# A new written order for the first two chunks of a fused attention and MLP kernel

## The chip, the cores and the metric

The kernel runs on one core of one Trainium2 chip. Its time is the device time of one execution in microseconds (us); of several runs the median is taken. A core has five engines with an instruction queue each, worked off in order: TensorE (PE: matrix products, with weight loads shown as PEld), VectorE (DVE), ScalarE (ACT), GpSimd (POOL) and SyncE (SP, which here only issues transfers). They meet at semaphores: an instruction waits until another engine or a transfer has raised one.

## The reference

Attention whose keys are limited to the query's hash bucket, then a layer norm and an MLP with a residual, on 4 batches of 8 heads, 768 positions, 64 dimensions a head:

```python
q_bits = (np.einsum('bhsd,dk->bhsk', q, proj) > 0).astype(np.int64)
k_bits = (np.einsum('bhsd,dk->bhsk', k, proj) > 0).astype(np.int64)
mask = q_bucket[:, :, :, None] == k_bucket[:, :, None, :]
scores = scale * np.matmul(q, k.transpose(0, 1, 3, 2))
scores = np.where(mask, scores, -1000000000.0)
attn = np.exp(scores - np.max(scores, axis=-1, keepdims=True))
attn = attn / (np.sum(attn, axis=-1, keepdims=True) + 1e-09)
x = np.matmul(attn, v)                                # heads side by side: (4, 768, 512)
xn = (x - mu) / np.sqrt(var + 1e-06) * g_ln
out = x + np.maximum(xn @ w_ch1, 0.0) @ w_ch2         # 512 -> 2048 -> 512
```

## The kernel before, in words

The rows are cut into 12 chunks of 256 queries, three for each batch. For a chunk, `att_units` (line 502) makes 12 units, three for each pair of heads. A unit has four steps: `scores` (four matmuls of 256 columns, L531, into one of two PSUM buffers named sc), `exps` (one ScalarE activation over 128x1024, L541, into one of three buffers), `values` (eight matmuls a head block, L566; before the first unit of a pair one more, L555) and `divide` (VectorE, L584 and L593). `mlp_steps` makes the MLP of a chunk: statistics (L612, L613), centring (L618), a transposition of the result (in the opening on TensorE, L654, and a copy out of PSUM, L662 or L664; later by a transfer), eight up products (L675), each rectified on VectorE (L685) or ScalarE (L687), and the down products (L716). From the third chunk on, a planner (`interleave`) lays the MLP of the chunk before and the preparation of the next batch between the units of attention.

The first two chunks have no such planner. Nothing is prepared when the kernel starts, and `first_two` (line 848) issues the work in an order that stands written out as a text, `opening` (line 835). Each word of it is one call; the digits say which head, unit or step, the last letter which engine (a ScalarE, d or p VectorE, g GpSimd). Since every engine works its own queue in order, the order of the words is the order in each queue, and a word that waits holds up everything behind it on its engine. The words, by the `table` at line 882:

- K: 26 matmuls that do no work while the first loads are under way (L861). J: a copy of the projection on VectorE (L875). G, LG: takes a PSUM buffer for a hash.
- T h: four transposes for head h (three blocks of two keys' columns and one of queries) into one PSUM bank (L231). A trailing d (T1d) picks the other of two banks, which are those of the values as well.
- E h: scales that bank into SBUF, a whole 128x512 copy on ScalarE (L248) or VectorE (L250). The hash reads the result.
- C h.p: casts one half (64 partitions) into the operands' place: from PSUM on VectorE with letter p (L275), from E's result on GpSimd (L269) or ScalarE (L267).
- H j: hashes heads 2j and 2j+1 (16 short matmuls, L288 for the first pair and L312 for the others). B h: compares the hash with zero (VectorE, L339), which gives the bits. O h: copies the odd half of the bits into place (L269, L267).
- LT, LE, LC, LH, LB, LO: the same for the four late blocks of queries (LT0 and LT2 of the first four heads, LT1 and LT3 of the others), whose columns are loaded last.
- S u, X u, V u, D u: scores, exps, values, divide of unit u (25 of them: two chunks and one unit of the third).
- vc: cast of the values (L432). su, sd: their sums on TensorE (L456) and the split of these on VectorE (L463, L464).
- w0 to w3: GpSimd issues the weights' and the next batch's loads (L749, L140, L756, L186). na, bl, op: the next batch's narrowing (L357), block transposes (L362) and transposing transfers (L380).
- n, ns, nr, xt, xe, U, R: the first chunk's statistics, centring, scale, transposition, its copy, up products and rectifications.

T's bank is read by E and, where the letter is p, by C. The framework puts a wait between instructions on two engines that touch the same tile in PSUM, in the order in which they were issued. The scaled copies of four heads share four buffers (qkT), three more lie in a buffer (spare, line 242) that the next batch's narrowing takes over.

Of the kernel before, what the change touches and what calls it, by code (L numbers as in the profile page):

```python
# [30 lines left out]
def kernel(  # L31
# [796 lines left out]
    def chunk_tile():  # L828
# [4 lines left out]
    mlp = {0: mlp_steps(*chunks[0], xs[0])}  # L833

    opening = """
        K26 G1 J0 T0 E0a C0.1p T1d E1a H0 T2d C1.0g B0 B1 C1.1g C0.0g T3 O0g E2a E3a S0 C3.0p X0 H1
        O1g C2.1g C3.1p S1 vc0 S2 C2.0g X1 B3 O3a T4d B2 O2g T5 E4d E5a su0 sd0 S3 T7d E7d G2 C4.1g
        X2 T6 H2 B5 C5.1a V0 E6a S4 X3 V1 w0 X4 V2 C4.0g LT0 S5 C5.0g O5g B4 G3 H3 X5 LE0d O4g C6.1a
        V3d D2 B6 vc1 S6 B7 X6 C7.1g LT1d S7 V4 V5 LE1a su1 LC0.1g X7 D5 LG0 S8 C6.0g O6g LT3d sd1
        LH0 LE3d S9 V6 LB1 C7.0g LB0 X8 O7g w1 LT2 LC0.0g X9 V7 LO0g S10 V8 LG1 S11 LE2d X10 LH1 D8  # L840
        LB3 V9d LC1.0g S12 V10 X11 LO1g V11 S13 w2 X12 X13 LC1.1g LB2 V12 S14 X14 S15 D11 V13 n0 S16
        X15 n1 V14 X16 S17 ns0 ns1 LO3g na0 xt0 V15 xe0a V16 S18 U0 X17 w3 LO2a U1 X18 R0d V17 R1d
        U2 D14 LC2.0a na1 S19 U3 R2d V18 D17 bl0 S20 X19 S21 R3a bl2 X20 V19 U4 R4a V20 U5 bl1
        LC2.1g X21 D20 S22 op0 U6 S23 R5d X22 U7 V21d V22 X23 LC3.0g R7a S24 nr0 R6d V23 X24 D23
        LC3.1a bl3
    """

    def first_two():
# [364 lines left out]
```

## Time and profile before

| | |
|---|---|
| three runs, median (lowest to highest) | 304.77 us (304.59 to 305.6) |
| the profiled execution | 304.0 us, of which 302.1 span (first to last instruction) and 1.9 around it |
| busy: TensorE, ScalarE, VectorE, GpSimd | 293.6, 216.7, 179.4, 91.0 us |
| exps (L541) | 144, 159.4 us in all, 1112 ns each |
| granted TensorE clock | 1.00 |

The views of the profile: the page with sums over the whole execution; the chain of waits, which goes back from the last instruction to what released each step; busy time in stretches; and the timeline, one row for each run of equal instructions on an engine: start and length in us, engine, line, operation, tiles written and read, count, and in brackets how long the engine was idle before it and what ended that. A wait for several semaphores is put down to the one that came last. Matmuls are pipelined, so their length is not their pace: a run of equal ones is read from the start of the first to the start of what follows.

### The profile page before, as it was taken

How to read it: one execution, taken by the hardware profiler on the slowest of the kernel's cores; microseconds unless marked ns; L12 is line 12 of the kernel's file. 1: busy time of each engine (PE TensorE's matmuls, PEld its weight loads, DVE VectorE, ACT ScalarE, POOL GpSimd, SP SyncE). 2: the span in 40 equal slices, each digit the busy share in tenths (PEclk: the TensorE clock that was granted, in tenths of full speed). 3: DMA queues.
4: the chain of work that ended last, by engine and by line, in shares of the span. 5: the costliest groups of instructions: out<-in, count | busy, mean ns of one | idle time of the engine just before them, and what ended most of it. 6: DMA issues, size and time to landing. Idle time of an engine off the chain costs nothing.

```text
span 302.1 us, 7969 instructions
## 1 busy us (share of the span) xinstructions
PE 293.6 (97%) x3279; PEld 224.4 (74%) x3306; DVE 179.4 (59%) x420; ACT 216.7 (72%) x271; POOL 91.0 (30%) x119
## 2 busy tenths in 40 slices
PE   8899999999999999999999999999999999999994
PEld 6677886687697687688687678678688688687574
DVE  3788568745387487455855874734744645645422
ACT  3899987777887786787797788688698578575020
POOL 3999811593031072520730830100100100100200
PEclk9999999999999999999999999999999999999999
DMA  7999999988586948955596354420310200200302
GB/s 216 364 223 275 239 240 233 134 186 166 135 292 112 237 134 150 254 174 146 149 248 180 85 95 108 51 80 2 55 52 2 70 37 2 72 37 2 105 2 75
DMA packets 58713, 40.93 MB, mean 135 GB/s; under 512 B 38672, under 2 KB 53520, under 8 KB 58672
## 3 DMA queue, kind: packets, MB, share of 16 engines
q1 hardware_dynamic: 53808, 30.80, 43.8%
q0 software_dynamic: 4288, 8.91, 12.5%
q10 hardware_dynamic: 576, 0.66, 0.7%
q8 instruction: 27, 0.44, 0.6%
q14 instruction: 14, 0.11, 0.1%
HBM read 27.98 MB, written 6.88 MB: 115 GB/s over the span
## 4 chain that ended last, share of the span: by engine, by line
PE 91%; ACT 3%; DVE 2%; issue 1%; DMA 1%; POOL 1%; ACTq 0%; SPq 0%
PE hp L675 28%; PE o L716 23%; PE sc L531 20%; PE av L566 11%; PE hash L398 3%; ACT ex L541 3%; PE tpose L231 1%; PE o L698 1%; DMA xnT<-xn 1%; PE wakep L861 1%; POOL slots L269 1%; PE hash L312 1%; PE sums L456 0%; DVE xn L618 0%; DVE stats L612 0%
## 5 line engine op out<-in xcount | busy, mean ns | idle before, releaser
L541 ACT ACTIVATE ex<-sc,expb 128x1024 bf16<-128x1024 f32 x144 | 159.4, 1112 | 53.2 <-PE sc L531 52.0
L675 PE MATMUL hp<-xnT,w_sb 128*128 128x256 bf16 x768 | 98.3, 272 | 0.1
L716 PE MATMUL o<-w_sb,hbuf 128*128 128x512 bf16 x341 | 89.8, 379 | 1.2
L531 PE MATMUL sc<-slots 70*128 70x256 bf16 x576 | 86.5, 272 | 1.9 <-POOL slots L269 1.0
L675 PEld LDWEIGHTS <-w_sb 128*128 128x128 bf16 x768 | 71.8, 97 | 8.9 <-DMA xnT<-xn 0.6
L566 PEld LDWEIGHTS <-ex 128*128 128x128 bf16 x1152 | 54.0, 98 | 14.4 <-issue 1.2
L531 PEld LDWEIGHTS <-slots 70*128 70x128 bf16 x576 | 51.8, 97 | 16.7 <-issue 2.0
L685 DVE TENSOR_SCALAR hbuf<-hp 128x512 bf16<-128x512 f32 x49 | 33.7, 688 | 44.4 <-PE hp L675 44.3
L566 PE MATMUL av<-vaug,ex 128*128 128x65 bf16 x1152 | 58.6, 194 | 0.2 <-ACT ex L541 0.2
L629 POOL TENSOR_SCALAR rs<-mv 128x2 f32<-128x2 f32 x12 | 8.6, 717 | 152.0 <-DVE mv L613 151.9
L716 PEld LDWEIGHTS <-hbuf 128*128 128x128 bf16 x368 | 33.5, 97 | 25.4
L687 ACT ACTIVATE hbuf<-hp 128x512 bf16<-128x512 f32 x47 | 27.9, 593 | 17.1 <-PE hp L675 17.1
L721 DVE SCALAR_TENSOR_TENSOR x<-o,rs,x 128x512 f32<-128x512 f32 x23 | 17.1, 742 | 22.0 <-PE o L716 21.9
L593 DVE TENSOR_TENSOR x<-av,rc 128x256 f32<-128x256 f32 x48 | 20.4, 424 | 1.6
L586 DVE TENSOR_SCALAR rc<-av 128x4 f32<-128x4 f32 x36 | 5.7, 157 | 24.8 <-PE av L566 24.8
L618 DVE SCALAR_TENSOR_TENSOR xn<-x,mv,gbc 128x512 bf16<-128x512 f32 x24 | 18.1, 760 | 0.7
L612 DVE BATCH_NORM_STATS2 stats<-x 128x6 f32<-128x512 f32 x24 | 16.5, 688 | 0.4
L587 DVE TENSOR_TENSOR av<-av,vsum 128x256 f32<-128x256 f32 x36 | 15.6, 433 | 1.2
L357 POOL CAST nat<-qnat 128x1536 bf16<-128x1536 f32 x6 | 8.9, 1482 | 21.2 <-DMA qnat<-in_q_dram 12.5
L432 POOL CAST vaug<-vnat 128x1536 bf16<-128x1536 f32 x8 | 11.7, 1468 | 7.5 <-DMA vnat<-in_v_dram 7.3
L211 ACT ACTIVATE knat<-knat 128x768 f32<-128x768 f32 x16 | 13.4, 836 | 0.0
L211 ACT ACTIVATE qnat<-qnat 128x768 f32<-128x768 f32 x16 | 13.3, 833 | 0.0
(87 smaller groups left out, 203.9 us busy)
## 6 DMA issues: line engine op xcount, KB each, us to landing
out_dram<-x SPq DMA_DIRECT2D x23, 256.0 KB
vnat<-in_v_dram SPq DMA_DIRECT2D x6, 768.0 KB
w_sb<-in_moe_w_ch_dram POOLq DMA_DIRECT2D x4, 1024.0 KB, 13.3
knat<-in_k_dram SPq DMA_DIRECT2D x10, 384.0 KB
qnat<-in_q_dram SPq DMA_DIRECT2D x8, 384.0 KB
slots<-slots SPq DMA_DIRECT2D x12, 192.0 KB
qnat<-in_q_dram POOLq DMA_DIRECT2D x2, 768.0 KB, 12.9
knat<-in_k_dram POOLq DMA_DIRECT2D x2, 768.0 KB, 15.2
```

Of the source, the lines that this page charges most:

```text
L211: nc.scalar.activation(src, src, AF.Square, accum_out=sq[:, a, col : col + 1],)
L531: nc.tensor.matmul(sc[:, i, :], key_block(h, kj), query_blocks(h),)
L541: nc.scalar.activation(ex, sc, AF.Exp, bias=expb[:, 1:2] if b else expb[:, 0:1], scale=scale if b else scale / Q_SCALE,)
L566: nc.tensor.matmul(av[:, h - ha, qi, :], state[g][:, i, qi * P : (qi + 1) * P], va[:, h, kj, :], start=(b > 0 and (g, i, qi) == (0, 0, 0)) ...
L593: nc.vector.tensor_tensor(xv, num, rc.unsqueeze(3).to_broadcast([P, 2, TT, D]), op=AOP.mult)
L612: nc.vector.bn_stats(stats, x[:, i, :])
L618: nc.vector.scalar_tensor_tensor(xn[:, :, i, :], x[:, i, :].rearrange("p (o d) -> p o d", d=P), mv[:, i, 0:1], gbc.rearrange("p (o d) -> p ...
L675: nc.tensor.matmul(hp[:, i, :], w1_sb[:, dt, nt * P : (nt + 1) * P], st["xnT"][:, dt, :], start=(dt == 0), stop=(dt == ND - 1),)
L685: nc.vector.tensor_scalar_max(dst, src, 0.0)
L687: nc.scalar.activation(dst, src, AF.Relu)
L716: nc.tensor.matmul(o2, st["h"][:, nt, i * P : (i + 1) * P], w2_sb[:, nt, :], start=(nt == 0), stop=(nt == NH - 1),)
L721: nc.vector.scalar_tensor_tensor(x[:, i, :], o2, st["rs"][:, i : i + 1], x[:, i, :], op0=AOP.mult, op1=AOP.add,)
```

## The change

Only the text `opening` is rewritten. It has the same 207 words, in another order, and for some of them the letter changes, so that another engine makes the copy: VectorE now casts C0.0, C2.0, C2.1, C5.1 (and no longer C0.1, C3.1), ScalarE casts C0.1, C1.0, C3.1, C4.1 (no longer C5.1, C6.1, LC3.1 and the odd bits O3, LO2, which go to GpSimd but for C5.1). The scaling copies E7 and LE2 go to ScalarE, LE1 to VectorE; the copy of the transposed chunk (xe) goes from ScalarE to VectorE; of the rectifications R0, R2, R6 go to ScalarE, R4 and R7 to VectorE. T4 to T7, LT0, LT3 and the values V0, V9, V12, V15, V18 take the other of their two banks. Among the late queries, LT2 now comes ahead of LT1 and LT0.

```diff
     opening = """
-        K26 G1 J0 T0 E0a C0.1p T1d E1a H0 T2d C1.0g B0 B1 C1.1g C0.0g T3 O0g E2a E3a S0 C3.0p X0 H1
-        O1g C2.1g C3.1p S1 vc0 S2 C2.0g X1 B3 O3a T4d B2 O2g T5 E4d E5a su0 sd0 S3 T7d E7d G2 C4.1g
-        X2 T6 H2 B5 C5.1a V0 E6a S4 X3 V1 w0 X4 V2 C4.0g LT0 S5 C5.0g O5g B4 G3 H3 X5 LE0d O4g C6.1a
-        V3d D2 B6 vc1 S6 B7 X6 C7.1g LT1d S7 V4 V5 LE1a su1 LC0.1g X7 D5 LG0 S8 C6.0g O6g LT3d sd1
-        LH0 LE3d S9 V6 LB1 C7.0g LB0 X8 O7g w1 LT2 LC0.0g X9 V7 LO0g S10 V8 LG1 S11 LE2d X10 LH1 D8
-        LB3 V9d LC1.0g S12 V10 X11 LO1g V11 S13 w2 X12 X13 LC1.1g LB2 V12 S14 X14 S15 D11 V13 n0 S16
-        X15 n1 V14 X16 S17 ns0 ns1 LO3g na0 xt0 V15 xe0a V16 S18 U0 X17 w3 LO2a U1 X18 R0d V17 R1d
-        U2 D14 LC2.0a na1 S19 U3 R2d V18 D17 bl0 S20 X19 S21 R3a bl2 X20 V19 U4 R4a V20 U5 bl1
-        LC2.1g X21 D20 S22 op0 U6 S23 R5d X22 U7 V21d V22 X23 LC3.0g R7a S24 nr0 R6d V23 X24 D23
-        LC3.1a bl3
+        K26 G1 J0 T0 C0.0p E0a T1d E1a H0 T2d B0 C1.0a C1.1g C0.1a B1 O0g T3 C2.0p S0 E2a E3a C3.1a
+        H1 X0 O1g S1 S2 C3.0p B3 X1 vc0 B2 O2g C2.1p T4 su0 X2 E4d sd0 T5d O3g C4.0g C5.1p G2 S3 E5a
+        T7 H2 T6d C4.1a E7a V0d E6a B5 V1 w0 S4 vc1 X3 X4 B4 V2 D2 G3 H3 O4g S5 LT2 S6 LT1d LE2a V3d
+        B7 B6 su1 O5g LE1d V4 C5.0g X5 X6 sd1 LT0d LG0 C6.0g S7 V5 C7.1g X7 LE0d S8 LH0 D5 O6g C7.0g
+        C6.1g LB1 LB0 X8 S9 V6 V7 X9 O7g LT3 S10 w1 X10 V8 LC0.1g LG1 S11 LE3d X11 LH1 D8 LO0g V9
+        LC0.0g S12 LB2 LC1.0g w2 V10 LB3 V11 S13 D11 X12 n0 S14 X13 n1 LO1g LC1.1g LC3.1g V12d X14
+        S15 ns1 ns0 V13 X15 S16 V14 S17 xt0 X16 V15d X17 S18 xe0d V16 w3 X18 U0 D14 S19 LO3g bl2 V17
+        R0a U1 R1d X19 S20 U2 U3 na0 X20 V18d R2a LC2.0a U4 V19 S21 na1 R3a X21 LC2.1g U5 V20 bl1
+        bl3 S22 R4d D17 LO2g X22 S23 R5d V21d U6 U7 V22 LC3.0g S24 bl0 X23 D20 R6a R7d op0 V23 D23
+        nr0 X24
     """
```

## The prediction

> **What bounds the kernel now.** I read the page first, then the chain of waits for the opening, then the queues of ScalarE, VectorE and GpSimd for the same stretch, since the change lies wholly in the opening (the first two of twelve chunks).
>
> ```profile
> span 302.1 us, 7969 instructions
> PE 91%; ACT 3%; DVE 2%; issue 1%; DMA 1%; POOL 1%; ACTq 0%; SPq 0%
> ```
>
> TensorE carries 91% of the chain that ended last. The list of matmuls is the same before and after, so the question is only where TensorE waits. The busy time in four stretches of the opening shows it (span, then busy time of PE, PEld, DVE, ACT, POOL):
>
> ```profile
> 5.00:9.40 4.40, 3.23 (x40) 1.82 (x46) 3.00 (x5) 2.12 (x5) 3.08 (x6) 1.00 1.04 360
> 9.40:23.30 13.90, 13.80 (x201) 10.56 (x197) 11.51 (x28) 13.01 (x15) 13.23 (x19) 1.00 1.11 277
> 23.30:33.10 9.80, 8.98 (x147) 7.01 (x146) 7.24 (x17) 9.52 (x10) 8.28 (x12) 1.00 1.10 286
> 33.10:45.00 11.90, 11.88 (x149) 10.77 (x149) 7.70 (x15) 10.54 (x13) 5.48 (x8) 1.00 1.22 223
> ```
>
> Before 9.4 us TensorE waits for the first keys to be copied, hashed and placed; from 9.4 to 23.3 us it hardly waits; from 23.3 to 33.1 us ScalarE is busy 9.52 of 9.80 us with the exps and is the bound; from 33.1 us TensorE has no pause. The chain of waits tells the same (start, us, what):
>
> ```profile
> 4.00 0.87 PE tpose L231 x4
> 4.89 1.13 ACT qkT L248 x2
> 6.08 0.61 POOL slots L269
> ...
> 8.08 0.62 POOL slots L269
> 8.74 0.61 PE sc L531 x4
> 9.38 1.12 ACT ex L541
> 10.54 0.60 PE sc L531 x4
> 11.14 0.88 PE tpose L231 x8
> 12.01 0.69 PE sums L456 x6
> ...
> 14.20 0.59 PE hash L312 x16
> 14.80 0.22 PE av L555
> ...
> 23.31 1.12 ACT ex L541
> ...
> 31.56 0.46 PE xnTp L654 x8
> 32.05 1.03 ACT xnT L662
> 33.12 1.91 PE hp L675 x16
> ...
> 279.65 1.31 DVE xn L618 x2
> ```
>
> From 10.54 to 23.3 us it is TensorE almost alone, without a gap to take up a delay; then exps to 30.97, the transposed copy (L662) and the first up products at 33.12 (U0 below); behind that TensorE to the last normalisation at 279.65. So **a time lost before 23 us returns only where ScalarE's stage gives it back, and what U0 is late the end is late.**
>
> **The change, worked through.** It changes who does several copies, and in which order. The one edit that matters most is small: the blocks of keys that a transpose T leaves in PSUM are read twice, by a scaling copy E (L248 or L250; the hash H reads its result) and by a cast C (L275 when VectorE takes it straight from PSUM). Before, E came first and C second:
>
> ```profile
> 4.62 0.17 DVE L875 COPY proj<-proj 64x6 f32<-64x6 f32 x1 [2.87 <-DMA proj<-in_proj_dram]
> 5.52 0.69 DVE L275 TENSOR_SCALAR slots<-tpose 64x512 bf16<-64x512 f32 x1 [0.74 <-ACT qkT L248]
> 6.65 0.55 PE L231 MATMUL tpose<-identf,knat 128*128 128x128 f32 x3
> 6.80 1.41 DVE L339 TENSOR_SCALAR slots<-hash 38x512 bf16<-38x512 f32 x2 [0.58 <-PE hash L288]
> 7.34 1.09 ACT L248 ACTIVATE qkT<-tpose 128x512 f32<-128x512 f32 x2 [1.33 <-PE tpose L231]
> ```
>
> The second row is the witness: VectorE stood idle 0.74 us until ScalarE's copy had ended, though both only read the block. Two readers on two engines are put one behind the other. The changed order writes C0.0p before E0a, C2.0p before E2a and C5.1p before E5a, and in the changed program these three ScalarE copies wait for VectorE, where all seven scaling copies of before wait for TensorE. So now the copy that leads to the hash, and on ScalarE everything queued behind it, exps included, stands behind a VectorE cast.
>
> [...]
>
> Step 1, heads 0 and 1. T0 is done at 4.87, the copy of the projection at 4.62 + 0.17 = 4.79. So C0.0p takes 4.89 to 5.58, and E0a with E1a (1.13 us together) 5.62 to 6.75, where they ended at 6.02: 0.73 us late. T2 followed the end of that pair by 0.63 us (6.65), the compares by 0.78 (6.80), so T2 comes at 7.38 and B0, B1 (1.41 us) at 7.53 to 8.94. The scores S0 need the odd bits O0 (0.62 us on GpSimd) after B0, which ends at 8.24: S0 at about 8.94, 0.2 us late. That is small because GpSimd now has one cast instead of three ahead of O0 (C1.0 goes to ScalarE, which has nothing else then, C0.0 to VectorE).
>
> Step 2, heads 2 and 3. T2 lies ready at about 7.9 us, but C2.0p stands on VectorE behind both compares: 8.96 to 9.65. E2a and E3a (1.09 to 1.13 us) follow at 9.69 to 10.82 instead of 7.34. Then comes the ScalarE cast C3.1a, 0.63 us by the row below, and only then the first exp X0, at about 11.45 instead of 9.38. H1 ends 0.63 us after the pair, S1 goes at 11.45 and fills the second score buffer; S2 must wait until X0 has read the first, 11.45 + 1.12 = 12.57, and starts at 12.60 instead of 10.54. **TensorE is 2.06 us late.** Bounds: 0.2 (S0's lateness) if only step 1 counted; 2.35 (E2a, 9.69 against 7.34) if nothing of it were made good.
>
> ```profile
> 11.61 0.69 DVE L250 TENSOR_SCALAR spare<-tpose 128x512 f32<-128x512 f32 x1
> 12.74 0.43 DVE L463 CAST vsplit<-sums 128x260 bf16<-128x260 f32 x1 [0.43 <-PE sums L456]
> 13.20 0.43 DVE L464 TENSOR_TENSOR vsplit<-sums,vsplit 64x260 bf16<-64x260 f32 x1
> 14.06 0.63 ACT L267 ACTIVATE slots<-spare 64x512 bf16<-64x512 f32 x1
> 14.59 0.57 ACT L248 ACTIVATE qkT<-tpose 128x512 f32<-128x512 f32 x1
> ```
>
> Step 3, heads 4 and 5. From S2 TensorE does S2, T4, su0, T5, S3, T7: five groups of 0.44 (two transposes are 0.88 in the chain) and the sums' 0.69, 2.89 us, to 15.5. On VectorE, T4 (done 13.6 with its own latency) lets E4d run 13.65 to 14.34, then the split of the sums (12.74 to 13.63 before, 0.89 us) to about 15.25, then C5.1p to 15.96. E5a follows to 16.57 and H2 ends 0.63 us later, 17.2; T6 adds 0.44, so the first values V0 start at 17.65. Before they started at 14.80. From S2 to V0 it was 4.26 us and is 5.05: **0.79 more.** Bounds: 0 if VectorE came through earlier, 1.3 if the compares of H1 push E4d and all behind it by one cast (0.69) less the 0.2 that TensorE lost to T4's late load.
>
> Step 4, to U0. The middle of the opening has the same work on TensorE. ScalarE's row of eight exps and the copy behind it are:
>
> ```profile
> 23.31 8.61 ACT L541 ACTIVATE ex<-sc,expb 128x1024 bf16<-128x1024 f32 x8 [0.60 <-PE av L566]
> L664 DVE COPY xnT<-xnTp x1: 692/692/692, 53.0 to 53.0; 128x1024 bf16<-128x1024 bf16 x1
> ```
>
> The copy of xnT goes from ScalarE (1.03) to VectorE, which has room (7.24 of 9.80): 1.03 - 0.69 = **0.34 less.** If VectorE had no room it would gain 0; at best the whole 1.03.
>
> Hidden: the odd bits O3 and LO2 and the casts C5.1, C6.1 that leave ScalarE, and the few that come, lie in 9.4 to 23.3 us beside TensorE work; without that cover each costs 0.6. The order of the late blocks (LT0, LT2, LT1, LT3) changes behind loads that have landed by then. GpSimd's DMA issues move too, the first weights first of all:
>
> ```profile
> 13.30 1.74 POOL L749 DMA_DIRECT2D w_sb<-in_moe_w_ch_dram  x2
> w_sb<-in_moe_w_ch_dram POOLq DMA_DIRECT2D x4, 1024.0 KB, 13.3
> ```
>
> They were issued from 13.30 to 15.04 and landed some 13.3 us later, at 28.3; U0 needs them at 33.12. Two microseconds later are covered by 4.8, and U0 moves as well; without that cover each microsecond would count in full.
>
> Sum: 2.06 + 0.79 - 0.34 = 2.51 us. The profiled execution took 304.0 us (302.1 span and 1.9 around it), so 306.5 on its own scale; the median of the three runs is 304.77, and 304.77 + 2.51 gives **307.3 us.** The bounds together run from 0.2 + 0 - 1.03 = -0.8 to 2.35 + 1.3 - 0 = 3.65.
>
> **The rivals** need two rows more:
>
> ```profile
> 1.05 2.95 PE wakep L861 x26
> L687 ACT ACTIVATE hbuf<-hp 128x512 bf16<-128x512 f32 x47 | 27.9, 593 | 17.1 <-PE hp L675 17.1
> ```
>
> - The opening is set by ScalarE's sum (the other side: not slower). Its stage from 23.3 to 33.1 has 97% busy. Counting the two orders, ScalarE gains one scaling copy (0.57) and one rectification (0.59), and loses one cast (0.63) and the xnT copy (1.03): 0.50 us less. If ScalarE worked without pause from the first exp and the early loss were hidden, 304.3. It decides once ScalarE's queue, and not the hash chain, is what the first exps wait for. Against it: ScalarE is busy 2.12 of 4.40 us before 9.4, it waits there for keys.
> - The waits don't hold the copies up, because two readers overlap. Steps 1 and 2 then leave the 0.2 of S0; S2, with X0 at about 9.6, is not later than that: 0.2 + 0.79 - 0.34 = 0.65, so 305.4. Against it: the 0.74 us.
> - ScalarE's stage gives back more: TensorE is idle 0.82 of 9.80 us there, and if its lateness of 2.85 ate into that, 2.51 - 0.82 gives 306.5. Against it: ScalarE arrives as late as TensorE, having lost 2 us of exps.
> - TensorE loses clock in the pauses, which come in a row: 0.73 before H0, 1.4 before H1, 0.7 before S2, 1.4 before H2. That there is a half pace the rows show: the first matmuls took 2.95/26 = 0.113 us each for 128 columns, the eight of L654 0.46/8 = 0.058. A second stretch like that first one would do 2.95/2 = 1.5 us of work less: 308.8. Against it: the granted clock is 1.00 in every stretch above, and before 9.4 us the pauses of 1.17 us cost no clock.
>
> [...]
>
> **How the numbers follow.** The forecast, both held copies deciding, 0.79; stage gives back more, 0.06; readers overlap, 0.05; ScalarE's sum, 0.04; clock lost, 0.06. The forecast's own range is 306.3 to 308.3, its two large terms off by up to 40% together (0.95 us). Down to the third rival and to the sum of the upper bounds the range is 305.8 to 308.5; it leaves out most of three rivals with 0.15. A difference of 0.3% (0.9 us) is about what a measurement of this kernel can tell from none. Slower than 305.7: forecast, third and fourth rival, 0.91. Within: the second rival and half of the first, 0.07. Faster: 0.02.
>
> **What would show it.** Right: E0a near 5.6 us with VectorE as what released it; E2a near 9.7 and the first exp near 11.4; scores S2 near 12.6; the copy ahead of H2 near 16.0, again released by VectorE; first values at 17.6; U0 at 35.6; last normalisation at 282.2; TensorE's busy time unchanged. Step 2 is wrong if the first exp comes before 10.5 us; step 3 if V0 follows S2 by under 4.5 us; step 4 if U0 is later against V0 than the 18.3 us of before. The prediction as a whole is wrong if U0 is less than 1 us later.

## The result, and the profile after

| | changed kernel | kernel before, same chip |
|---|---|---|
| first comparison: median (lowest to highest), runs | 307.05 us (306.43 to 307.6), 8 | 305.06 us (304.59 to 306.29), 8 |
| ratio, 95% interval | 1.0057 [1.0039, 1.0075] | |
| second comparison (the last experiment) | 306.9 us (306.48 to 308.25), 12 | 305.01 us (303.87 to 308.23), 17 |
| ratio, 95% interval | 1.0049 [1.0019, 1.0079] | |
| profiled execution, its span, granted clock | 307.19, 305.4, 1.0 | 304.0, 302.1, 1.0 |

An execution more than 1.5% longer than the fastest of its kernel counts as slow, and all ratios, and the medians of the runs with an extra load below, leave such executions out.

The change makes the kernel slower by 0.5 to 0.6%, to 307.05 us where 307.3 was predicted. The page of the changed kernel, with the chain that ended last by engine:

```profile
span 305.4 us, 7998 instructions
PE 90%; DVE 5%; ACT 2%; DMA 1%; POOL 1%; issue 1%; SPq 0%; ACTq 0%; POOLq 0%
```

VectorE's share of the chain has grown from 2 to 5%. Busy time in the same four stretches as before (span; PE, PEld, DVE, ACT, POOL; then granted clock, DMA share, GB/s):

```profile
5.00:9.40 4.40, 3.25 (x32) 1.87 (x30) 2.43 (x4) 2.34 (x4) 1.66 (x3) 1.00 1.03 351
9.40:23.30 13.90, 12.01 (x154) 8.57 (x153) 9.85 (x23) 11.67 (x15) 10.55 (x15) 1.00 1.04 260
23.30:33.10 9.80, 9.19 (x152) 7.07 (x150) 8.39 (x23) 8.75 (x10) 9.23 (x15) 1.00 1.07 270
33.10:45.00 11.90, 11.74 (x152) 10.44 (x152) 8.39 (x14) 9.96 (x12) 7.99 (x11) 1.00 1.28 212
```

The stretch from 9.4 to 23.3 us was the one in which TensorE hardly waited, 13.80 of 13.90; now it has 12.01, and every other engine has less as well. Who waits there is in the chain of waits of the opening (start, us, what):

```profile
4.90 0.69 DVE slots L275
5.61 0.61 ACT qkT L248
6.26 1.20 PE hash L288 x16
7.49 0.68 DVE slots L339
8.21 0.69 DVE slots L339
8.93 0.69 DVE slots L275
9.65 0.61 ACT qkT L248
10.30 1.23 PE hash L312 x16
...
13.07 0.69 DVE slots L275
13.79 0.69 DVE spare L250
...
15.31 0.70 DVE slots L275
16.04 0.61 ACT spare L248
16.69 0.74 PE hash L312 x12
...
282.75 1.31 DVE xn L618 x2
```

Three times the chain goes from a VectorE cast out of the transpose's bank (L275) to the ScalarE copy out of the same bank (L248) and from there to a hash: at 5.61, 9.65 and 16.04. The prediction had 5.62, 9.69 and 16.0. The timeline gives the releaser of each, and the rows further down on which the sum stood:

```profile
5.61 1.08 ACT L248 ACTIVATE qkT<-tpose 128x512 f32<-128x512 f32 x2 [2.44 <-DVE slots L275]
9.65 1.09 ACT L248 ACTIVATE qkT<-tpose 128x512 f32<-128x512 f32 x2 [1.65 <-DVE slots L275]
12.59 0.60 PE L531 MATMUL sc<-slots 70*128 70x256 bf16 x4 [0.60 <-ACT ex L541]
13.02 0.49 PE L231 MATMUL tpose<-identf,knat 128*128 128x128 f32 x3
16.04 0.60 ACT L248 ACTIVATE spare<-tpose 128x512 f32<-128x512 f32 x1 [1.50 <-DVE slots L275]
17.82 0.27 PE L555 MATMUL av<-vsplit,epsk 128*128 128x260 bf16 x1
34.54 0.61 PE L654 MATMUL xnTp<-ident,xn 128*128 128x128 bf16 x8
35.19 0.69 DVE L664 COPY xnT<-xnTp 128x1024 bf16<-128x1024 bf16 x1 [0.78 <-PE xnTp L654]
36.03 1.04 PE L675 MATMUL hp<-xnT,w_sb 128*128 128x256 bf16 x8
```

S2 starts at 12.59 (before 10.54: 2.05 late), the first values at 17.82, and the last normalisation at 282.75 (279.65: 3.10 late). The 14.80 that the prediction has for the first values before comes from the chain of waits; in the timeline, from which the 17.82 is read, they start at

```profile
14.73 0.29 PE L555 MATMUL av<-vsplit,epsk 128*128 128x260 bf16 x1
```

so that they are 3.09 us late (3.02 against the chain's figure). Nearly the whole loss has arisen by 17.8 us in the trace, and on balance nothing behind gives any of it back.

### The profile page after: what moved, and what is told of

It reads as the page before. It is cut to its first block, busy times and chain, and to the rows that moved or that the text cites. A ratio compares the mean times of both kernels' runs of the same rounds, so it can differ in the third digit from the quotient of the medians.

```text
span 305.4 us, 7998 instructions
## 1 busy us (share of the span) xinstructions
PE 296.5 (97%) x3306; PEld 224.6 (74%) x3306; DVE 180.2 (59%) x421; ACT 215.7 (71%) x271; POOL 90.3 (30%) x118
## 4 chain that ended last, share of the span: by engine, by line
PE 90%; DVE 5%; ACT 2%; DMA 1%; POOL 1%; issue 1%; SPq 0%; ACTq 0%; POOLq 0%
PE hp L675 27%; PE o L716 24%; PE sc L531 19%; PE av L566 11%; PE hash L398 3%; DVE slots L339 1%; ACT ex L541 1%; PE o L698 1%; PE hash L312 1%; DMA xnT<-xn 1%; PE wakep L861 1%; DVE slots L275 1%; PE tpose L231 1%; POOL slots L269 1%; DVE xn L618 0%
## 5 line engine op out<-in xcount | busy, mean ns | idle before, releaser
L716 PE MATMUL o<-w_sb,hbuf 128*128 128x512 bf16 x368 | 92.9, 379 | 0.0
L531 PE MATMUL sc<-slots 70*128 70x256 bf16 x576 | 86.7, 272 | 2.0 <-ACT ex L541 1.2
L531 PEld LDWEIGHTS <-slots 70*128 70x128 bf16 x576 | 51.7, 97 | 17.7 <-issue 4.6
L685 DVE TENSOR_SCALAR hbuf<-hp 128x512 bf16<-128x512 f32 x48 | 33.0, 688 | 43.2 <-PE hp L675 43.0
L618 DVE SCALAR_TENSOR_TENSOR xn<-x,mv,gbc 128x512 bf16<-128x512 f32 x24 | 17.8, 750 | 0.8
L432 POOL CAST vaug<-vnat 128x1536 bf16<-128x1536 f32 x8 | 11.8, 1473 | 7.5 <-DMA vnat<-in_v_dram 7.4
```

The costliest lines, as they stand in the source:

```text
L531: nc.tensor.matmul(sc[:, i, :], key_block(h, kj), query_blocks(h),)
L618: nc.vector.scalar_tensor_tensor(xn[:, :, i, :], x[:, i, :].rearrange("p (o d) -> p o d", d=P), mv[:, i, 0:1], gbc.rearrange("p (o d) -> p ...
L685: nc.vector.tensor_scalar_max(dst, src, 0.0)
L716: nc.tensor.matmul(o2, st["h"][:, nt, i * P : (i + 1) * P], w2_sb[:, nt, :], start=(nt == 0), stop=(nt == NH - 1),)
```

## The experiments

Theory: the three ScalarE copies held behind VectorE casts are the whole loss. Rival: the rest of the new order (compares, odd bits, casts, letters) costs as much or more. The first four kernels are the changed one with one, or all, of the three pairs turned round again.

**All three copies first.**

```diff
-        K26 G1 J0 T0 C0.0p E0a T1d E1a H0 T2d B0 C1.0a C1.1g C0.1a B1 O0g T3 C2.0p S0 E2a E3a C3.1a
-        H1 X0 O1g S1 S2 C3.0p B3 X1 vc0 B2 O2g C2.1p T4 su0 X2 E4d sd0 T5d O3g C4.0g C5.1p G2 S3 E5a
+        K26 G1 J0 T0 E0a C0.0p T1d E1a H0 T2d B0 C1.0a C1.1g C0.1a B1 O0g T3 E2a C2.0p S0 E3a C3.1a
+        H1 X0 O1g S1 S2 C3.0p B3 X1 vc0 B2 O2g C2.1p T4 su0 X2 E4d sd0 T5d O3g C4.0g E5a C5.1p G2 S3
```

> The changed order with three words moved: E0a ahead of C0.0p, E2a ahead of C2.0p, E5a ahead of C5.1p; all letters and all other words stay. Theory (the three scaling copies held behind VectorE casts are the whole loss): first exp back at 9.0 to 9.6 us, first values near 14.6, first up products at 32.8 to 33.3, time 304.3 to 305.2, ratio to the kernel before 0.997 to 1.001. Rival A (the rest of the new order costs, or ScalarE's letters): no change against the changed kernel, ratio 1.005 to 1.007. Rival B (half each): 306, ratio 1.003.

Measured: 305.0 us (303.69 to 308.07, 12 runs), ratio to the kernel before 0.9999 [0.9963, 1.0035]. Within that interval the whole loss is gone, with all else of the change in place.

**One copy first** (`E0a C0.0p`, `E2a C2.0p` or `E5a C5.1p` alone).

> The changed order with E0a alone moved ahead of C0.0p. Theory: the first copy back at 4.9 us, T2 and everything behind it 0.7 us earlier: first exp at 10.6, first up products 0.7 us earlier, time 306.3, ratio 1.003 to 1.005. Rival A: no change, 1.005 to 1.007. If only the second pair decides: copy early, but first exp still at 11.4 and no change in time.

> The changed order with E2a alone moved ahead of C2.0p. Theory: E2a at 8.0 instead of 9.65 us, first exp 1.6 us earlier at 9.8, of which the first values keep some 1.2 (third pair's wait unchanged): time 305.8, ratio 1.001 to 1.003. Rival A: no change, 1.005 to 1.007.

> The changed order with E5a alone moved ahead of C5.1p. Theory: first exp stays at 11.4; the copy goes at 14.9 instead of 16.04 us, first values at 16.7 instead of 17.8, time 1.0 us less, 306.0, ratio 1.002 to 1.004. Rival A: no change, 1.005 to 1.007.

| turned round | median (lowest), runs | ratio to before | last normalisation against the changed kernel |
|---|---|---|---|
| E0a | 306.56 (305.6), 11 | 1.0045 [1.001, 1.0079] | 0.81 us earlier |
| E2a | 305.74 (305.32), 12 | 1.0036 [1.0019, 1.0052] | 0.40 us earlier |
| E5a | 306.07 (305.62), 12 | 1.0051 [1.0033, 1.0069] | 0.91 us earlier |

The intervals of the ratios overlap, so the times alone rank nothing; each median lies below the changed kernel's, by 0.49, 1.31 and 0.98 us, and their lowest runs by 0.83, 1.11 and 0.81 us, which add up to 2.75 beside the 2.74 of all three (306.43 less 303.69). Two ratios lie above what was expected, 1.0036 (1.001 to 1.003) and 1.0051 (1.002 to 1.004), and by its interval E5a alone could as well have changed nothing (rival A). It is the traces that show what each does. In the timeline with E0a first:

```profile
4.88 1.08 ACT L248 ACTIVATE qkT<-tpose 128x512 f32<-128x512 f32 x2 [1.72 <-PE tpose L231]
8.92 1.09 ACT L248 ACTIVATE qkT<-tpose 128x512 f32<-128x512 f32 x2 [1.65 <-DVE slots L275]
11.85 0.60 PE L531 MATMUL sc<-slots 70*128 70x256 bf16 x4 [0.60 <-ACT ex L541]
```

Released by the transposes, the first copy comes 0.73 us earlier, and so do E2a (9.65 to 8.92) and S2 (12.59 to 11.85), though E2a is still held. With E2a first:

```profile
5.45 1.08 ACT L248 ACTIVATE qkT<-tpose 128x512 f32<-128x512 f32 x2 [2.28 <-DVE slots L275]
7.87 1.08 ACT L248 ACTIVATE qkT<-tpose 128x512 f32<-128x512 f32 x2
10.80 0.60 PE L531 MATMUL sc<-slots 70*128 70x256 bf16 x4 [0.25 <-ACT ex L541]
13.30 0.69 DVE L250 TENSOR_SCALAR spare<-tpose 128x512 f32<-128x512 f32 x1 [0.94 <-PE tpose L231]
```

S2 comes 1.79 us earlier, 0.16 of it because this execution's first copy did (5.45 instead of 5.61), but only 0.40 reaches the end of this execution: T4, which could now start at 11.4, waited for its keys until 12.15, and E4d (L250) for T4. With E5a first, E5a goes from 16.04 to 14.77 and V0 from 17.82 to 16.64.

**The fault put into the old order.** The kernel before, with one word moved.

```diff
-        K26 G1 J0 T0 E0a C0.1p T1d E1a H0 T2d C1.0g B0 B1 C1.1g C0.0g T3 O0g E2a E3a S0 C3.0p X0 H1
+        K26 G1 J0 T0 C0.1p E0a T1d E1a H0 T2d C1.0g B0 B1 C1.1g C0.0g T3 O0g E2a E3a S0 C3.0p X0 H1
```

> The kernel before with one word moved: the compare C0.1p ahead of the eviction E0a, which is what the change does to this pair, and nothing else of the change. Theory: E0a goes from 4.88 to 5.6, the scores S0 and all behind come 0.7 us later, 0.2 to 0.3% over the kernel before. Rival (the fault needs the rest of the new order): within 0.1%.

(What is moved, C0.1p, is a cast; this expectation and that of the repeated first run call such casts compares.) Measured: 304.87 us (304.26 to 306.23, 12 runs), ratio 0.9997 [0.9972, 1.0022]; the expected 0.2 to 0.3% can't be told from nothing by it. In the trace the mechanism is there:

```profile
4.85 0.69 DVE L275 TENSOR_SCALAR slots<-tpose 64x512 bf16<-64x512 f32 x1
5.58 1.08 ACT L248 ACTIVATE qkT<-tpose 128x512 f32<-128x512 f32 x2 [2.41 <-DVE slots L275]
9.40 0.60 PE L531 MATMUL sc<-slots 70*128 70x256 bf16 x4 [1.00 <-POOL slots L269]
```

E0a is at 5.58, S0 at 9.40 (before 8.74), and the last normalisation at 280.31, 0.66 us later than before's. The lowest run is 0.70 above the lowest of the kernel before (303.56). So an opening that is later by 0.7 in the trace has the same median. That may be noise, since the interval reaches 0.67 us. A part of it is on record: the mean granted clock of every execution is 0.994 or less in 4 of the 23 of the kernel before and in 1 of these 12, and 0.997 or more in all others, and of these others the medians are 304.46 and 304.83.

**The input's copy alone (step 4).**

```diff
-        X15 n1 V14 X16 S17 ns0 ns1 LO3g na0 xt0 V15 xe0a V16 S18 U0 X17 w3 LO2a U1 X18 R0d V17 R1d
+        X15 n1 V14 X16 S17 ns0 ns1 LO3g na0 xt0 V15 xe0d V16 S18 U0 X17 w3 LO2a U1 X18 R0d V17 R1d
```

> The kernel before with one letter changed: the copy of the transposed input (xe0) on VectorE instead of ScalarE, and nothing else. The prediction's step 4: 0.34 us faster (0.1%), from nothing to 1.03 us (0.3%). Rival, by the changed kernel's trace, where nothing came of it: within 0.05%, because the up-projection's first product waits less but the exponentials set the end of that stretch.

Measured: 304.44 us (303.53 to 307.98, 12 runs), ratio 1.0003 [0.997, 1.0036], which decides nothing. Its timeline, against xnTp at 31.40 and U0 at 33.12 before:

```profile
32.40 0.61 PE L654 MATMUL xnTp<-ident,xn 128*128 128x128 bf16 x8
33.05 0.69 DVE L664 COPY xnT<-xnTp 128x1024 bf16<-128x1024 bf16 x1 [1.03 <-PE xnTp L654]
33.90 1.91 PE L675 MATMUL hp<-xnT,w_sb 128*128 128x256 bf16 x16
```

This execution is 1.00 us later than before's from 23.3 us on (0.32 of it at S0, 9.06 instead of 8.74), but U0 follows xnTp by 1.50 us instead of 1.72: **0.22 us gained,** and the last normalisation, at 280.44, is 0.79 later, not 1.00. The medians of the executions with a clock of 0.997 or more, 304.15 (10 runs) and 304.46 (19), agree with a small gain, but that choice was made afterwards.

**When the loads land.** The chain of waits of the first experiment's profiled execution, a long one of 308.07 us, starts with a load that the kernel before's doesn't have:

```profile
3.97 8.50 DMA knat<-in_k_dram
...
12.61 1.24 PE tpose L231 x4
...
16.00 0.85 PE sc L531 x4
```

The second half's first keys landed at 3.97 + 8.50 = 12.47. In this execution T4 could have started near 10.6 (S2 at 10.11 and its 0.44) and waited; and then TensorE ran at half its pace (four score matmuls in 0.85 us, where before they took 0.44). Two theories for the spread, 303.56 to 309.43 in 91 executions of the kernel before (median 304.86, 23 of them over 306): the landing of these loads, or TensorE's clock. An extra load ahead of the first values puts the later loads back; what is computed stays the same. First 768 KB of it, in both kernels, then 384 KB:

```diff
             elif args[0] == "v":
+                if args[1] == 0:
+                    part("k", 1, 0, 4, 0, NC, nc.sync)
                 tiles[args[1]]["v"] = load_values(0, args[1])
```

> The kernel before, with one more load of 768 KB (the second half's keys, loaded again by the listed loads afterwards) put on SyncE's queue ahead of the first values, so that those values and all loads behind them land about 2.2 us later (what the first values' own load takes). Nothing computed changes. Theory (the old opening reads the second half's keys at once as they land, the new one has some 2 us to spare): T4 waits to about 12.6 instead of 10.9, and TensorE then runs at a reduced pace for some us; the time is 305.5 to 308.5, 0.6 to 1.5% over the kernel before. Rival (when the loads land plays no part, and the spread between executions has another cause): within 0.3% of the kernel before.

> The changed kernel with the same extra load. Theory: T4 stands at 13.0 there, after the keys have landed at about 12.5, so that nothing waits: 306.4 to 307.5, no more than 0.2% over the changed kernel, and level with or below the run of the old opening with late loads: the change's loss is gone when the loads are late. Rival (the loads' landing plays no part): the same distance of about 0.6 to 0.9% to the old opening with late loads as without the extra load. Second rival (the extra load slows everything, by contention in the memory): both late kernels rise by the same amount.

> The kernel before with half of the extra load of the runs before (384 KB of keys, loaded again later by the listed load). By the larger one, which put the second half's first keys from 10.1 to 14.1, they should land near 12.1, where the old opening's T4 stands at 10.9. Theory: the wait of 1.2 us and the reduced pace of TensorE behind it cost 2.5 to 4.5 us: median 307 to 309, lowest not under 306. Rival (the pace has nothing to do with the wait): only the wait, 1.2 us, lowest 304.8.

> The changed kernel with the same half load. Theory: the keys land near 12.1 and T4 stands at 13.07, so an execution without further lateness waits for nothing: lowest 306.4 to 306.9 as without the load, median 306.5 to 308.5, because executions in which the loads come another 2 us late now wait as well; so the two openings are level here. Rival (the larger extra load cost by contention, not by the wait): 1 us or more above the changed kernel already in the lowest run.

| extra load | kernel before | changed kernel |
|---|---|---|
| none | 304.62 us (17 runs, beside the 384 KB runs) | 306.96 us (20 runs of two comparisons) |
| 384 KB | 309.02 (308.45 to 313.03, 4), ratio 1.0162 [1.0092, 1.0231] | 308.17 (307.26 to 309.6, 6), ratio 1.0101 [1.0061, 1.0141] |
| 768 KB | 310.02 (308.21 to 311.7, 6), ratio 1.0162 [1.0124, 1.0201] | 310.5 (309.0 to 313.58, 5), ratio 1.0221 [1.0164, 1.0277] |

All ratios are to the unaltered kernel before. The 768 KB miss their expectations on both sides (305.5 to 308.5 and 306.4 to 307.5): in the profiles they came to 4 us, not 2.2, so that T4 waited in both orders (to 14.41 and 14.59), and nothing follows from them but that such a wait, with the lower clock that came in both profiles (0.986 and 0.994 in the mean), is dear. With 384 KB the keys landed near 12.2 in the old order, where the row below is T4; behind it this execution lost still more to the late queries, which landed at 22.90 there (11.34 and 11.56 in its chain of waits), since the extra load pushed them back as well (timeline):

```profile
12.20 0.90 PE L233 MATMUL tpose<-identf,knat 128*128 128x128 f32 x3 [1.06 <-DMA knat<-in_k_dram]
```

By the medians the old order pays 4.4 us for this, the upper end of the expected 2.5 to 4.5, and the new one 1.2. They are level within their spread, as was expected, since the ranges and the intervals of the ratios overlap. But the new one's lowest run, 307.26, isn't the expected 306.4 to 306.9 either; it is 0.83 above the changed kernel's lowest, short of the rival's 1 us or more but near it, so contention by the extra load isn't ruled out. The windows of 2 us (same columns as above) of its profiled execution, 308.75 us, show one reason, though not that of the lowest run, whose mean clock is 0.998; below them S2 and T4 in its timeline (two added lines make L531 L533 there, and L231 L233):

```profile
10.00:12.00 2.00, 1.68 (x20) 0.72 (x21) 1.18 (x3) 1.94 (x4) 0.54 (x1) 1.00 0.64 226
12.00:14.00 2.00, 1.42 (x8) 1.30 (x8) 1.71 (x4) 2.00 (x3) 1.75 (x3) 0.71 1.15 323
14.00:16.00 2.00, 2.00 (x12) 1.62 (x10) 1.11 (x2) 0.55 (x1) 1.30 (x3) 0.50 0.84 253
```

```profile
12.58 0.81 PE L533 MATMUL sc<-slots 70*128 70x256 bf16 x4 [0.60 <-ACT ex L543]
13.19 0.85 PE L233 MATMUL tpose<-identf,knat 128*128 128x128 f32 x3
```

T4 followed S2 without a wait, as the theory had it; but from S2 on the granted clock was down to one half, after the same waits as in the changed kernel's own profile, where it stayed at 1.00. So both theories hold a part: the old order waits for late keys, and the clock can fall in either.

**The three copies first, and the changed kernel, again.**

> The kernel of the first run again (the three copies ahead of the compares), for a profile of an execution whose loads land early. Theory: E0a at 4.9, E2a near 7.5, first scores of the third piece (S2) at 10.5, T4 at 10.9 without a wait, clock 1.0 and 303.7 to 304.3; median 304.5 to 305.5. Rival (the clock loss belongs to this order, not to the late loads): a clock of 0.987 again with early loads.

> The changed kernel unaltered, in twelve more executions beside the kernel before. Two things are asked. First the ratio: 1.0039 to 1.0075 on record. Second the spread: the kernel before runs from 303.6 to 309.4 in the runs so far. Theory (the old opening, which reads the second half's keys at 10.9, pays for loads that land at 11 to 12.5, and the new one, which reads them at 13.07, does not): the changed kernel stays within 306.4 to 307.8 again and has no tail. Rival (the spread comes from TensorE's clock, which any pause can set back): the changed kernel too has some executions at 308 to 310.

The first: 305.14 us (304.26 to 307.93, 12 runs), ratio 1.0011 [0.9981, 1.0042], so once more level with the kernel before. Its profile was wanted for early loads and caught another late one (keys at 11.84, T4 at 11.97, clock 0.986, 307.86 us); that this clock comes with early loads too, as its rival says, stays untested. The windows show how long the half clock lasted, and a short one, put first, when it began:

```profile
11.00:11.20 0.20, 0.00 (x0) 0.00 (x0) 0.19 (x1) 0.20 (x1) 0.20 (x1) 0.66 1.03 369
...
10.00:12.00 2.00, 0.63 (x5) 0.35 (x4) 1.65 (x4) 2.00 (x3) 1.12 (x1) 0.77 1.06 369
12.00:14.00 2.00, 2.00 (x9) 1.39 (x10) 0.69 (x1) 0.31 (x1) 1.52 (x4) 0.50 1.07 368
...
16.00:18.00 2.00, 2.00 (x22) 0.90 (x21) 0.69 (x1) 1.22 (x2) 1.76 (x2) 0.53 0.97 125
18.00:20.00 2.00, 2.00 (x49) 1.87 (x49) 1.53 (x5) 1.29 (x2) 0.17 (x1) 1.00 1.12 212
```

A mean of 0.66 over the first window puts the fall at 11.06 us. S2 had ended at 10.96 (10.36 and 0.60), so the wait for the keys was 0.1 us old and can't be what brought the clock down in this execution. The six microseconds from T4 on at half clock are 3 us of work, and the run is 3.6 above the lowest of its twelve. The second: 306.9 us, and eleven of twelve runs within 306.4 to 307.8 as the theory had it, one at 308.25, as its rival had it. In its profiled execution the loads landed later than in the first one (GpSimd's cast of the first values waited for them, at 10.13 instead of 9.64 without a wait, and the keys landed at 11.09 instead of 10.38):

```profile
10.13 1.47 POOL L432 CAST vaug<-vnat 128x1536 bf16<-128x1536 f32 x1 [0.57 <-DMA vnat<-in_v_dram]
12.58 0.60 PE L531 MATMUL sc<-slots 70*128 70x256 bf16 x4 [0.60 <-ACT ex L541]
17.82 0.27 PE L555 MATMUL av<-vsplit,epsk 128*128 128x260 bf16 x1
```

S2, E5a (16.04) and V0 stand where they stood, to 0.01 us, and the last normalisation is at 282.75 again.

## Why the prediction was right, step by step

- **The mechanism.** Right: in all three pairs the two readers of the bank, on two engines, went one after the other, in written order. E0a starts at 5.61, behind the end of the cast (4.90 and 0.69), and written first at 4.88, where the cast follows at 5.51; E2a goes from 9.65 to 7.87 and E5a from 16.04 to 14.77. Turning three pairs round gives back everything (0.9999). The second rival (readers overlap, 305.4) falls by the three releasers alone. The first rival, ScalarE's sum, falls too: the changed order gives ScalarE less to do, and from 9.4 to 23.3 us it is busy 11.67 instead of 13.01 us, waiting.
- **Step 1** (0.73 late) and **step 2** (2.06): right, E0a 5.61, E2a 9.65, first exp 11.42, S2 12.59, a loss of 2.05.
- **Step 3:** right in kind, mis-sized: V0 follows S2 by 5.23 us, not by the 5.05 of the sum. Before, that was 4.26 by the chain, which the sum took, and 4.19 by the timeline, so 0.97 or, like for like, 1.04 was lost instead of 0.79. E5a came on time (16.04), but not quite by the path of the sum, which had E4d wait for T4. T4 had ended at 13.62, and E4d started at 13.79, when C2.1p, behind the compares of H1 on VectorE (13.07 in the chain), had ended; the prediction has that queue only in its upper bound. That it cost no more than 0.14 is luck. The other part of that bound, 0.2 us for a late load of T4 before, isn't in the trace: T4's row shows no wait, and the keys had landed at 10.31. Of the missing 0.17 us, 0.07 are the copy's (0.04 in its start, 0.60 instead of 0.57 in its length) and 0.10 the hash's and T6's behind it (17.82 - 16.64 = 1.18 instead of 1.08).
- **Step 4:** mis-sized where it acts, and nothing of it is left at the end. From xnTp to U0 both the copy alone (1.50 us) and the changed order (36.03 - 34.54 = 1.49) take 0.22 to 0.23 less than the 1.72 of before, not 0.34: the copy had ended at 35.88, and values, scores and values fill that stretch on TensorE (1.50 in the chain), which the sum didn't weigh. By its own sign the step holds, U0 stands 18.21 us behind V0 (before 18.32 by the chain, 18.39 by the timeline). But in the changed order the last normalisation is 246.72 behind U0 instead of 246.53, and so 264.93 behind V0 (264.85, or 264.92 by the timeline). The written bound for VectorE without room, no gain, is what came, though not for that reason. Which edit behind U0 takes the gain back was not tried.
- **The third rival** (ScalarE's stage gives more back, 306.5): no. The last normalisation is later by 3.10, V0 by 3.02 to 3.09. (The prediction puts the lower end of its wide range, 305.8, "down to the third rival", whose time is 306.5; nothing hangs on it.)
- **The fourth rival** (clock lost in the pauses, 308.8): not in either profile of the changed kernel (1.00), but the clock can fall in that order, as its 384 KB run shows; that a pause makes it fall is not shown. One stretch of 3.4 us at half clock, as there, makes a mean clock of 0.994 over 305 us, and that is on record for 2 of the 20 executions without an extra load, 307.61 and 308.25.
- **The sum.** 2.51 us was forecast and the traces lose 3.10: 2.05 in step 2, 1.04 in step 3, and nothing comes back in step 4. The medians lose less, 1.99 and 1.89 us, or by the ratios 305.06 x 0.0057 = 1.7 us and 305.01 x 0.0049 = 1.5. The prediction added its sum to the median, as if every execution of the kernel before were like the profiled one, and so two errors cancelled: the sum was 0.6 too small, and the kernel before's median execution has already lost part of what the change costs. That 307.3 came so near is in part luck. The kernel before has its lowest run at 303.56 and its median at 304.86, 1.30 apart; the changed kernel has 306.43 and 306.96, 0.53 apart. The difference of the lowest, 2.87, is near the traces' 3.10. Shown are pieces: in the old order and the restored one T4 waits when the keys land at 11.8 to 12.5, and half clock came in three such profiles, at 0.1 to 0.6 us into the wait (not in the one with E2a first, after 0.75 us of waiting), so that the wait is not shown to be its cause; in the changed order T4 stands at 13.02 and keys that land 0.7 us later move nothing. The clock's part can be counted, since each execution's mean clock is on record: 22 of the 91 executions of the kernel before have 0.994 or less (median 306.76), 7 of the 24 of the restored order, and 2 of the 20 of the changed kernel. Of the 23 over 306 us of the kernel before 19 are among them, so half clock makes most of its tail. It makes little of the gap of the medians: without these executions they are 304.60, 304.74 and 306.89, 2.29 apart over all comparisons, but in the second comparison, which ran both kernels side by side, 304.95 and 306.76, 1.81 apart and no more than the 1.89 of all. What makes up the rest to 3.10 stays open, since only profiled executions show their loads.

## What to carry to other kernels

Where two engines read one PSUM bank, write first the reader that the chain needs: a cast on another engine, written one word earlier, cost its whole length here (0.69 of the 0.73 us at E0a) and the time until that engine came to it (1.27 us in all at E5a). Three of them cost 2.0 us here between the medians, and 2.7 between the lowest runs. Take a profiled execution's difference for what it is: when a load lands within a microsecond of its reader, as at T4 before (10.31 and 10.97), the median of that kernel can hold waits that its profile doesn't show, and an edit that makes the opening later also makes it less exposed. A letter that shortens a copy is worth no more than what the path gives through: 0.34 on paper was 0.22 where it acts, and with the rest of the change nothing at the end.

## What had not been expected of the hardware

The second half's first keys landed up to 2.2 us apart between executions with the same loads: at 12.47 and 11.84 us in two profiles of one kernel, where the cast of the first values had waited for its load until 11.56 and 10.88, and at 10.23 in that of the cast put ahead in the old order. What decides it stays open. The end differs as well: the two profiles of the changed kernel agree to 0.01 us up to the last VectorE instruction, which ends at 301.92 and 301.91, but their spans are 305.4 and 304.6, so that 0.8 us between two spans can lie in the storing of the result alone.

The granted clock fell to 0.50 for 3.4 us in the two profiles with 384 KB and for 6.8 us in the two of the three copies first, counted from the clocks of their windows, and the mean clocks of the two profiles with 768 KB (0.994 and 0.986) are like theirs (0.993 and 0.994, 0.986 and 0.987). In some of them no long pause came before it: in the 384 KB run of the changed order TensorE was busy 1.68 of the 2 us before 12, and had paused for 0.60 ahead of S2. The same waits left it at 1.00 in two other executions, the profiled ones of the changed kernel. What sets it off, and what its length, no run shows.
